# Top-k attention and a squared-ReLU feed-forward on one core: weights in fewer, earlier loads, two early steps changed over sooner, and another order of the tail

## The chip, the core and the metric

The kernel runs on one core of one Trainium2 chip. The metric is the device time of one execution in microseconds (us). The core has five instruction streams that run beside each other and meet at semaphores: PE (TensorE, matrix products, with weight loads shown as PEld), DVE (VectorE), ACT (ScalarE), POOL (GpSimd) and SP (SyncE, which here only issues transfers). Transfers run on 16 DMA engines, which all issuing queues share.

## The reference, cut to what matters

```
scores = q @ k^T / 8                        # 8 batches x 8 heads, 576 rows, 64 wide, float32
kth    = the 32nd largest score of each row
attn   = softmax(scores where scores >= kth)
x      = (attn @ v), heads side by side     # 4608 tokens x 512
h      = relu(x @ w_in)                     # 512 x 2048
out    = (h * h) @ w_out                    # 2048 x 512, float32 out
```

## The kernel before

**Steps.** The 64 heads are taken as 32 pairs (`pairs`). A pair has four 128-row pieces for each head and a rest of 64 rows, and a step works on two such 128-row tiles at once. There are U = 144 steps, numbered u from 0. The loop over u is written out by hand as a pipeline, and every instruction is pinned to program order on its engine (`pin`), so that the order in the code is the order of each queue. A transfer queue is also in order: a transfer that waits holds back the ones behind it.

**One step.** `scores(u+1)` multiplies on PE into two PSUM tiles (`sc_a`, `sc_b`), and ACT copies them to `s` (L294). DVE does the search for the 32nd largest: `pairs_of` (L314, L315, and L317 in early steps) and `quads_of` (L323, L324) sort the 576 scores of a row into maxima and minima of pairs and quads in `cat`; `topk` then runs four rounds of "eight largest" (L374), with the found values replaced after the first three (L378). POOL computes the minima of the pairs from sums (`both` L338, `lesser` L347). `drop(u-1)` on POOL marks the scores below the limit in `gone` (L409) and adds that mark onto `s`, either by a POOL instruction (L411) or by a transfer that accumulates (L413). `exps(u-2)` on ACT (L417) makes the weights `w_two` from `s`, and `turn(u-2)` on SP (L426) transposes them by DMA into `wT`. `products(u-4)` on PE (L461) multiplies with the values, `invert` (L475, DVE) and `place` (L494, ACT) divide by the row sums and write the tokens `x_tok`.

**The constant EARLY (L350).** It is 11. For steps u < EARLY, DVE computes half of the pair minima itself (L317), POOL works on one half only, and ACT doesn't copy the far maxima (`copy_far`, L330). For u < EARLY - 2 the mark of `drop` is added by POOL (L411); from then on by the accumulating transfer (L413).

**Inputs.** `load_pair(i)` lists ten transfers for the q, k and v rows of pair i; `fetch(n)` issues the next n of them on SP. In a step, `fetch(4)` stands behind `turn(u-2)`. `prepare(u)` transposes q and k of the next pair when its due step (`due(i)`) has come: 5, 8, 11 for the pairs 1, 2, 3, each begun four steps ahead. The raw buffers are double.

**Weights.** `w_loads` holds eight loads of 64 partitions for `w_in` and four of 128 partitions for `w_out` (L744). `load_weights` issues them on POOL's queue, converting to bf16: two before `scores(0)`, one behind `lesser(0)`, and one at the end of each of the steps 0 to 8.

**Feed-forward.** When all heads of a 128-token tile are in, PE transposes it (L532), and `block` cuts its work in pieces: four `up` pieces (16 products each, L583, 512 columns of PSUM), each followed by `relu` (ACT, L590) and `square` (ACT L598, or DVE or POOL L596), and 16 products with `w_out` (L649), copied (L657) and stored. Pieces are spread over the steps by `dense`.

**The tail.** The last step's part of the loop (u = U - 2) and all that follows are ordered by hand. Four `up` pieces of the last tile but one (`one`, `two`, `three`, `four`) are left over; its 16 products with `w_out` are issued in parts by `one.bits(n)` (L631). The first two pieces share one PSUM tile of two banks (`two_banks`, named `sc_a`). The last steps' weights are masked on DVE (`mask`, L421), transposed on PE (`turn_by_tensor`, L443) and copied out of PSUM by `turned` (L448 on ACT, L450 on DVE). `tests` are small POOL instructions on `flags` (L384 to L386), which DVE reduces to `worst` (L936). Then the last tile is transposed (L532, copy L536), its four `up` pieces follow with parts of `one.bits` between them, and `halves` multiplies it with `w_out` in two halves (L615), copies them (L621, L623) and stores them (L625).

Of the kernel before, what the change touches and what calls it, by code (L numbers as in the profile page):

```python
# [13 lines left out]
f32 = mybir.dt.float32  # L14
# [9 lines left out]
def kernel(  # L24
# [9 lines left out]
    nc = tc.nc  # L34
# [10 lines left out]
    def pin(ins):  # L45
        tc.keep_in_program_order(ins)
        return ins
# [10 lines left out]
    ps_sc = while_scores.enter_context(tc.tile_pool(name="ps_sc", bufs=1, space=PSUM))  # L58
# [7 lines left out]
    w_in = const.tile([128, KH, d_ff], bf16, name="w_in")  # L66
# [61 lines left out]
    def fetch(n):  # L128
        while n and fetches:
            fetches.pop(0)[1]()  # L130
            n -= 1
# [130 lines left out]
    U = len(steps)  # L262
    first = {}
# [42 lines left out]
    def pairs_of(u):  # L306
# [43 lines left out]
    EARLY = 11  # L350
    held_m = {}
    tests = []

# [43 lines left out]
    def early_exps(u, x):  # L397
        d = st[u]
        if "e" not in d:
            d["e"], d["neg_e"] = {}, negate(u, 1)  # L400
        e = d["e"][x] = scp.tile([128, S], bf16, name="e", bufs=3)
        pin(nc.scalar.activation(e[:, :], d["s"][:, x, :], AF.Exp, bias=d["neg_e"][:, x, 0:1]))
# [12 lines left out]
    def exps(u, x):  # L415
        d = st[u]
        pin(nc.scalar.activation(w_two[u % 3][:, x, 0:S], d["s"][:, x, :], AF.Exp, bias=d["neg"][:, x, 0:1]))  # L417
# [62 lines left out]

    full = []

    def place(u, by_vec=False):
        for x, (i, c, a) in enumerate(steps[u]):
            b, pr = pairs[i]
            o, r = sums(u)[:, x, :], st[u]["r"]
            if c < 4:
                if (b, c) not in x_tok:
                    x_tok[b, c] = ffp.tile([128, 512], bf16, name="x_tok", bufs=8)
                h = 4 * (pr // 2) + 2 * a + pr % 2  # L490
                if by_vec:
# [12 lines left out]


    moves, ups, downs = [], [], []
    soon_moves = []
    late, tail = [], []
# [53 lines left out]
    homes = []  # L562
# [154 lines left out]
    def dense(u, x, later=False):  # L717
        if x == 0:
            ups_now[0] = 0
            while behind:  # L720
                behind.pop(0)()
            while fresh:
                fresh.pop(0)()
        if u in PLAN:
            for kind in PLAN[u][x]:
                take(kind, kind == "d")
            return
        for n in range(2 if u >= U - 20 and x == 0 else 1):
            if not piece(later, most_ups(u)) and n == 0 and shut[0] != u:
                idle_piece()  # L730


    w_loads = []
    for kh in range(KH):
        for e in range(2):
            rows = moe_w_in.rearrange("(t e a d) n -> t a e d n", t=2, e=2, a=2)[kh // 2, kh % 2, e]
            w_loads.append((w_in[64 * e:64 * e + 64, kh, :], rows))
    for g in range(4):
        rows = moe_w_out.rearrange("(f p) n -> p f n", p=128)[:, 4 * g:4 * g + 4, :]
        w_loads.append((w_out[:, 4 * g:4 * g + 4, :], rows))  # L740

    def load_weights(n):
        for to, rows in w_loads[:n]:
            pin(nc.gpsimd.dma_start(out=to, in_=rows))  # L744
        del w_loads[:n]
# [9 lines left out]
    def due(i):  # L755
        if i >= NP - 8:
            return 101 + 4 * (i - (NP - 8))
        return first[4 * (i // 4) + 3] - 1 - 4 * (3 - i % 4) if i >= 4 else 3 * i + 2

    def prepare(u):  # L760
        nonlocal coming
# [14 lines left out]
    load_weights(2)  # L776
    scores(0)
    both(0)
    copy_far(0)
# [8 lines left out]
    def ok(w):  # L788
        return 0 <= w < U
# [6 lines left out]
    def products(w):  # L796
        if ok(w):
            for x in range(2):
                weigh(w, x)
# [6 lines left out]
    for u in range(U):  # L806
        at_step[0] = u
        for x in range(2):
            if ok(u - 1) and not by_vector(u - 1, x):
                drop(u - 1, x)  # L810
        quads_of(u)
        topk(u, (0,))
        if u == U - 1:
            break
        if ok(u + 1):
            for i, c, a in steps[u + 1]:
                while coming <= i or (coming == i + 1 and soon):
# [12 lines left out]
        turn_x(u)  # L830
        moves.extend(soon_moves)
        soon_moves.clear()
        if ok(u - 2):
            exps(u - 2, 0)
            exps(u - 2, 1)
            turn(u - 2)
        fetch(4 if u < 12 else 3)
        topk(u, (1, 2))
        if u == U - 2:
            while behind:  # L840
                behind.pop(0)()
            take("d")
            products(u - 3)
            take("d")
        if ok(u + 1):
            pairs_of(u + 1)
            if u == U - 2:
                invert(u - 3)
            copy_far(u + 1)
            lesser(u + 1)  # L850
            if tests:
                pin(tests.pop(0)())
        if u == U - 2:
            place(u - 3)
            turn_x(u)
            take("d", True)
            early_exps(u, 1)
            moves.pop(0)()()
        topk(u, (3,))
        if casts_next:  # L860
            prepare(u)
        while after_far:
            after_far.pop(0)()
        after_far.extend(next_far)
        next_far.clear()
        if u < U - 2:
            dense(u, 0)
        st[u]["neg"] = negate(u, 2)
        if u < U - 2:
            dense(u, 1)  # L870
        load_weights(1)
# [3 lines left out]
    two_banks = ps_sc.tile([128, 2, 512], f32, name="sc_a")  # L875
    homes.extend(two_banks[:, z, :] for z in range(2))
    one, two = ups.pop(0)(), ups.pop(0)()
    behind.pop(0)()
    one.relu()
    three = ups.pop(0)()  # L880
    products(U - 4)
    four = ups.pop(0)()
    for x in range(2):
        exps(U - 3, x)
    turn(U - 3)
    exps(U - 2, 0)
    one.square(nc.gpsimd)
    two.relu()
    two.square(nc.gpsimd)
    early_exps(U - 1, 0)  # L890
    early_exps(U - 1, 1)
    topk(U - 1, (1, 2, 3))
    one.bits(4)
    three.relu()
    three.square(nc.gpsimd)
    while tests:
        pin(tests.pop(0)())
    mask(U - 2, 1)
    mask(U - 1, 0)
    mask(U - 1, 1)  # L900
# [7 lines left out]
    turned(U - 1, 0, False)  # L908
    products(U - 3)
    turn_by_tensor(U - 1, 1)  # L910
    turned(U - 1, 1, True)
    products(U - 2)
    invert(U - 4)
    invert(U - 3)
    invert(U - 2)
    place(U - 2, True)
    products(U - 1)
    invert(U - 1)
    place(U - 4)
    place(U - 3)  # L920
    place(U - 1, True)
    one.bits(2)
    by_hand.clear()
    late.append(True)
    turn_x(U)
    by_hand.append(True)
    move = moves.pop(0)()
    four.relu()
    late.clear()
    four.square()  # L930
    late.append(True)
    one.bits(2)
    move()
    tail.append(0)
# [4 lines left out]
    fifth.square()  # L939
    sixth = ups.pop(0)()  # L940
    sixth()
    one.bits(4)
    ups.pop(0)()()
    one.bits(4)
    ups.pop(0)()()
# [137 lines left out]
```

## Time and profile before

| | us |
|---|---|
| time, median of 3 runs | 905.44 (904.69 to 906.34) |
| the profiled execution's own time | 910.4 |
| its span, first to last instruction | 908.3 |
| busy: DVE | 878.8 (97%) |
| busy: POOL | 780.7 (86%) |
| busy: ACT | 761.2 (84%) |
| busy: PE | 683.6 (75%) |

The profile is of one execution. The views used are: the page's engine shares, the chain of work that ended last (followed back from the last instruction), the timelines of the engines (start, length, what, and in brackets the idle time before an instruction with what ended it), the windows (busy time of each engine in a stretch, the granted TensorE clock as a share of full speed, the share of the DMA engines, and GB/s), and the list of transfers with the median time from issue to landing. A DMA share over 1 means that packets of several queues stood open on the same engines. The profiled execution is 4.96 us above the median of the timed runs.

### The profile page before, as it was taken

Reading aid. Unit: us, or ns where it says so; the run is one execution under the profiler, and the core shown is the slowest. Engines: PE = TensorE matmul, PEld = TensorE weight load, DVE = VectorE, ACT = ScalarE, POOL = GpSimd, SP = SyncE. Lnnn points to the kernel's source line nnn. Section 1 sums busy time; section 2 is a strip of 40 time slices with the busy share of each in tenths; the row PEclk is TensorE's granted clock in tenths of the full one; section 3 lists DMA queues with packets and bytes.
Section 4 is the critical chain, followed back from the end, with each engine's and each line's share of the span. In section 5 each row is a group of like instructions: output and inputs, shape, how many; then the busy total and the mean of one; then the engine's idle time right before and its main releaser. Section 6 shows DMA issues by size and latency. Waiting matters only on the chain.

```text
span 908.3 us, 20985 instructions
## 1 busy us (share of the span) xinstructions
PE 683.6 (75%) x6264; PEld 426.1 (47%) x6264; DVE 878.8 (97%) x3629; ACT 761.2 (84%) x1755; POOL 780.7 (86%) x821
## 2 busy tenths in 40 slices
PE   6675867777777768777777677787777768887886
PEld 3332445444444445454454444554544444554554
DVE  6998999999999999999999999999999999999994
ACT  3564799889988898888998899888998888997894
POOL 7997889988898888888889888888898898899881
PEclk9999899999999998999998999989999899999998
DMA  7699898889988999899999988989799999787771
GB/s 146 105 165 147 189 187 196 191 193 209 196 189 172 193 206 195 186 184 200 198 190 196 197 195 195 193 194 202 183 202 199 198 205 211 151 169 164 166 162 40
DMA packets 290776, 164.78 MB, mean 181 GB/s; under 512 B 258144, under 2 KB 268640, under 8 KB 290656
## 3 DMA queue, kind: packets, MB, share of 16 engines
q1 hardware_dynamic: 267408, 80.29, 46.2%
q0 software_dynamic: 21904, 82.65, 40.7%
q8 instruction: 52, 0.85, 0.4%
q14 instruction: 68, 0.56, 0.2%
q10 hardware_dynamic: 1344, 0.43, 0.2%
HBM read 37.75 MB, written 9.44 MB: 52 GB/s over the span
## 4 chain that ended last, share of the span: by engine, by line
DVE 62%; issue 12%; ACT 7%; PE 4%; POOL 3%; DMA 2%; POOLq 0%; ACTq 0%
DVE m L374 25%; DVE cat L378 17%; DVE sc_b L314 6%; DVE most L315 4%; DVE cat L323 4%; DVE cat L324 4%; ACT s L294 1%; PE sc_b L285 1%; POOL cat L347 1%; DVE rsum L475 1%; ACT rl L590 1%; ACT x_tok L494 1%; DMA s<-gone_a 1%; ACT w_two_a L417 1%; PE gen L583 1%
## 5 line engine op out<-in xcount | busy, mean ns | idle before, releaser
L374 DVE MAX8 m<-cat 128x8 f32<-128x104 f32 (+3 forms) x1152 | 436.7, 419 | 0.0
L378 DVE MATCH_REPLACE8 cat<-m,cat 128x104 f32<-128x104 f32 (+2 forms) x864 | 261.5, 308 | 0.0
L338 POOL TENSOR_TENSOR cat<-s 128x576 int32<-128x576 int32 (+1 forms) x144 | 238.6, 1657 | 2.8 <-ACT s L294 2.8
L347 POOL TENSOR_TENSOR cat<-cat,most 128x576 int32<-128x576 int32 (+1 forms) x144 | 196.0, 1361 | 31.8 <-ACT most L330 10.7
L285 PE MATMUL sc_b<-qkT 64*128 64x288 f32 x512 | 109.9, 505 | 88.2 <-DVE cat L324 84.1
L285 PE MATMUL sc_a<-qkT 64*128 64x288 f32 x512 | 98.2, 457 | 89.4 <-DVE most L315 35.2
L583 PEld LDWEIGHTS <-w_in 128*128 128x128 bf16 x2304 | 144.8, 101 | 41.7 <-issue 19.0
L649 PE MATMUL dn_ps<-w_out,h 128*128 128x512 bf16 x544 | 155.9, 417 | 1.8 <-ACT wide L657 1.8
L583 PE MATMUL gen<-xT,w_in 128*128 128x128 bf16 x1984 | 135.6, 224 | 3.3 <-ACT xT L538 1.8
L409 POOL TENSOR_SCALAR gone_a<-s,neg 128x576 uint8<-128x576 f32 x143 | 107.1, 749 | 15.5 <-ACT neg L394 4.1
L409 POOL TENSOR_SCALAR gone_b<-s,neg 128x576 uint8<-128x576 f32 x142 | 106.3, 749 | 12.2 <-ACT neg L394 0.3
L294 ACT ACTIVATE s<-sc_b 128x576 f32<-128x576 f32 x144 | 93.4, 648 | 27.8 <-PE sc_b L285 24.0
L285 PEld LDWEIGHTS sc_a<-qkT 64*128 64x128 f32 x512 | 41.6, 188 | 116.8 <-issue 35.4
L294 ACT ACTIVATE s<-sc_a 128x576 f32<-128x576 f32 x144 | 91.3, 634 | 3.2 <-DVE cat L317 1.7
L285 PEld LDWEIGHTS sc_b<-qkT 64*128 64x128 f32 x512 | 45.0, 203 | 103.7 <-PE av_ps L461 62.5
L394 ACT ACTIVATE neg<-m 128x4 f32<-128x4 f32 (+1 forms) x145 | 29.9, 206 | 72.0 <-DVE m L374 70.6
L598 ACT ACTIVATE h<-rl 128x512 bf16<-128x512 f32 x137 | 86.3, 630 | 4.3
L590 ACT ACTIVATE rl<-gen 128x512 f32<-128x512 f32 x140 | 81.9, 585 | 1.8 <-PE gen L583 1.7
L461 PEld LDWEIGHTS <-wT 128*128 128x128 bf16 (+1 forms) x1600 | 55.3, 101 | 57.9 <-issue 45.8
L649 PEld LDWEIGHTS <-h 128*128 128x128 bf16 x544 | 52.5, 106 | 63.5 <-issue 29.9
L413 POOL DMA_DIRECT2D s<-gone_b x67 | 59.3, 885 | 22.0 <-DVE m L374 9.9
L413 POOL DMA_DIRECT2D s<-gone_a x66 | 58.3, 884 | 20.4 <-DVE m L374 10.8
(177 smaller groups left out, 1261.0 us busy)
## 6 DMA issues: line engine op xcount, KB each, us to landing
s<-gone_b POOLq DMA_DIRECT2D x67, 576.0 KB, 4.5
s<-gone_a POOLq DMA_DIRECT2D x66, 576.0 KB, 4.6
v_raw<-in_v_dram SPq DMA_DIRECT2D x64, 128.0 KB, 3.1
k_raw<-in_k_dram SPq DMA_DIRECT2D x63, 128.0 KB, 3.3
q_raw<-in_q_dram SPq DMA_DIRECT2D x63, 128.0 KB, 3.0
out_dram<-wide SPq DMA_DIRECT2D x31, 256.0 KB, 3.0
v_raw<-in_v_dram SPq DMA_DIRECT2D x64, 32.0 KB, 3.0
w_in<-in_moe_w_in_dram POOLq DMA_DIRECT2D x8, 256.0 KB, 4.5
```

Of the source, the lines that this page charges most:

```text
L285: pin(nc.tensor.matmul(out=ps[j][:, x, 0:HALF], lhsT=lhsT, rhs=rhs, start=True, stop=True))
L294: pin(nc.scalar.activation(s[:, :, j * HALF:(j + 1) * HALF], ps[j][:, :, 0:HALF], AF.Copy))
L338: pin(tt(less, s[:, :, 0:wide].bitcast(i32), s[:, :, HALF:HALF + wide].bitcast(i32), op=ALU.add))
L347: pin(tt(less, less, d["most"][:, 0:n_h, :, :].bitcast(i32).rearrange("p h x n -> p x h n"), op=ALU.subtract))
L374: pin(nc.vector.max(out=m[r][:, x, :], in_=part(r, x)))
L378: pin(nc.vector.match_replace(out=part(r, x), in_to_replace=m[r][:, x, :], in_values=part(r, x), imm_value=NEG))
L409: pin(nc.gpsimd.tensor_scalar(byte[:, x, :, 1], s[:, x, :], scalar1=d["neg"][:, x, 1:2], scalar2=-HUGE, op0=ALU.add, op1=ALU.mult))
L413: pin(nc.gpsimd.dma_start(out=s[:, :, :].rearrange("p x n -> p (x n)"), in_=byte[:, :, :, :].rearrange("p x n two -> p (x n two)").bitcast ...
L583: pin(nc.tensor.matmul(out=hp[:, n * n_rows:(n + 1) * n_rows], lhsT=w_in[:, kh, (f0 + n) * 128:(f0 + n + 1) * 128], rhs=xt(kh), start=(kh ...
L590: pin(nc.scalar.activation(kept["rl"][:, :], hp, AF.Relu))
L598: pin(nc.scalar.activation(h2, flat, AF.Square))
L649: pin(nc.tensor.matmul(out=op[:, :], lhsT=held["h2"][:, f, c * 128:(c + 1) * 128], rhs=w_out[:, f, :], start=(f == 0), stop=(f == NF - 1)))
```

## The change

It has four parts.

- **Loads.** `w_in` comes in four loads of 128 partitions and not eight of 64. One load is issued before `scores(0)`, one behind `lesser(0)` and one at the end of the steps 0 to 5, so all eight are out by step 5. In the steps 0 to 5 `fetch(4)` stands ahead of `exps(u-2)` and `turn(u-2)`. The due steps of the pairs 1, 2, 3 are 5, 7, 9.
- **EARLY is 9.** The steps 9 and 10 no longer have L317 on DVE; the marks of the steps 7 and 8 are added by transfer.
- **The first pieces of the tail.** `one` and `two` go to two PSUM tiles (`sc_a`, `sc_b`). `early_exps` of step U - 2 stands behind the last round of `topk`; `exps(U-2, 0)` behind `two.square`; `one.bits(8)` takes the place of `one.bits(4)`.
- **The last steps.** `three.relu`, `three.square` and the `tests` stand behind the products of the last steps, and `four.relu` and `four.square` (on POOL) behind `place`. The second half of the last step's weights is copied by DVE, not ACT; of the last step's two results one is placed by DVE and the other by ACT. `one.bits(4)` between the last tile's second and third `up` piece is gone.

```
--- before.py
+++ after.py
@@ -347,7 +347,7 @@
         pin(tt(less, less, d["most"][:, 0:n_h, :, :].bitcast(i32).rearrange("p h x n -> p x h n"), op=ALU.subtract))
 
     GROUP = 18
-    EARLY = 11
+    EARLY = 9
     held_m = {}
     tests = []
 
@@ -480,7 +480,7 @@
 
     full = []
 
-    def place(u, by_vec=False):
+    def place(u, by_vec=(False, False)):
         for x, (i, c, a) in enumerate(steps[u]):
             b, pr = pairs[i]
             o, r = sums(u)[:, x, :], st[u]["r"]
@@ -488,7 +488,7 @@
                 if (b, c) not in x_tok:
                     x_tok[b, c] = ffp.tile([128, 512], bf16, name="x_tok", bufs=8)
                 h = 4 * (pr // 2) + 2 * a + pr % 2
-                if by_vec:
+                if by_vec[x]:
                     pin(nc.vector.tensor_scalar(x_tok[b, c][:, h * 64:(h + 1) * 64], o[:, 0:64], scalar1=r[:, x, :], scalar2=None, op0=ALU.mult))
                 else:
                     pin(nc.scalar.activation(x_tok[b, c][:, h * 64:(h + 1) * 64], o[:, 0:64], AF.Copy, scale=r[:, x, :]))
@@ -732,9 +732,8 @@
 
     w_loads = []
     for kh in range(KH):
-        for e in range(2):
-            rows = moe_w_in.rearrange("(t e a d) n -> t a e d n", t=2, e=2, a=2)[kh // 2, kh % 2, e]
-            w_loads.append((w_in[64 * e:64 * e + 64, kh, :], rows))
+        rows = moe_w_in.rearrange("(t e a d) n -> t a e d n", t=2, e=2, a=2)[kh // 2, kh % 2]
+        w_loads.append((w_in[:, kh, :], rows))
     for g in range(4):
         rows = moe_w_out.rearrange("(f p) n -> p f n", p=128)[:, 4 * g:4 * g + 4, :]
         w_loads.append((w_out[:, 4 * g:4 * g + 4, :], rows))
@@ -755,7 +754,7 @@
     def due(i):
         if i >= NP - 8:
             return 101 + 4 * (i - (NP - 8))
-        return first[4 * (i // 4) + 3] - 1 - 4 * (3 - i % 4) if i >= 4 else 3 * i + 2
+        return first[4 * (i // 4) + 3] - 1 - 4 * (3 - i % 4) if i >= 4 else 2 * i + 3
 
     def prepare(u):
         nonlocal coming
@@ -773,7 +772,7 @@
     ones = const.tile([128, 1], f32, name="ones")
     pin(nc.gpsimd.memset(ones[:, :], 1.0))
     worst = const.tile([128, 1], f32, name="worst")
-    load_weights(2)
+    load_weights(1)
     scores(0)
     both(0)
     copy_far(0)
@@ -830,11 +829,14 @@
         turn_x(u)
         moves.extend(soon_moves)
         soon_moves.clear()
+        if u < 6:
+            fetch(4)
         if ok(u - 2):
             exps(u - 2, 0)
             exps(u - 2, 1)
             turn(u - 2)
-        fetch(4 if u < 12 else 3)
+        if u >= 6:
+            fetch(4 if u < 12 else 3)
         topk(u, (1, 2))
         if u == U - 2:
             while behind:
@@ -854,7 +856,6 @@
             place(u - 3)
             turn_x(u)
             take("d", True)
-            early_exps(u, 1)
             moves.pop(0)()()
         topk(u, (3,))
         if casts_next:
@@ -868,33 +869,29 @@
         st[u]["neg"] = negate(u, 2)
         if u < U - 2:
             dense(u, 1)
+        else:
+            early_exps(u, 1)
         load_weights(1)
 
     assert len(ups) == 4 and not downs and len(behind) == 1 and not fresh and not moves and not soon_moves
     by_hand.append(True)
-    two_banks = ps_sc.tile([128, 2, 512], f32, name="sc_a")
-    homes.extend(two_banks[:, z, :] for z in range(2))
-    one, two = ups.pop(0)(), ups.pop(0)()
+    homes.extend(ps_sc.tile([128, 2, 512], f32, name=name)[:, 0, :] for name in ("sc_a", "sc_b"))
+    one, two, three = (ups.pop(0)() for _ in range(3))
     behind.pop(0)()
     one.relu()
-    three = ups.pop(0)()
     products(U - 4)
     four = ups.pop(0)()
     for x in range(2):
         exps(U - 3, x)
     turn(U - 3)
-    exps(U - 2, 0)
     one.square(nc.gpsimd)
     two.relu()
     two.square(nc.gpsimd)
+    exps(U - 2, 0)
     early_exps(U - 1, 0)
     early_exps(U - 1, 1)
     topk(U - 1, (1, 2, 3))
-    one.bits(4)
-    three.relu()
-    three.square(nc.gpsimd)
-    while tests:
-        pin(tests.pop(0)())
+    one.bits(8)
     mask(U - 2, 1)
     mask(U - 1, 0)
     mask(U - 1, 1)
@@ -908,27 +905,29 @@
     turned(U - 1, 0, False)
     products(U - 3)
     turn_by_tensor(U - 1, 1)
-    turned(U - 1, 1, True)
+    turned(U - 1, 1, False)
     products(U - 2)
+    products(U - 1)
+    three.relu()
     invert(U - 4)
     invert(U - 3)
-    invert(U - 2)
-    place(U - 2, True)
-    products(U - 1)
-    invert(U - 1)
     place(U - 4)
     place(U - 3)
-    place(U - 1, True)
-    one.bits(2)
+    three.square(nc.gpsimd)
+    while tests:
+        pin(tests.pop(0)())
+    invert(U - 2)
+    place(U - 2, (True, True))
+    invert(U - 1)
+    place(U - 1, (True, False))
+    four.relu()
+    four.square(nc.gpsimd)
     by_hand.clear()
     late.append(True)
     turn_x(U)
     by_hand.append(True)
+    one.bits(2)
     move = moves.pop(0)()
-    four.relu()
-    late.clear()
-    four.square()
-    late.append(True)
     one.bits(2)
     move()
     tail.append(0)
@@ -939,7 +938,6 @@
     fifth.square()
     sixth = ups.pop(0)()
     sixth()
-    one.bits(4)
     ups.pop(0)()()
     one.bits(4)
     ups.pop(0)()()
```

More of the change, by code (lines that the diff above doesn't have):

```diff
@@ L349 @@
     GROUP = 18
-    EARLY = 11
+    EARLY = 9
     held_m = {}
@@ L481, with place @@
     full = []
-    def place(u, by_vec=False):
+    def place(u, by_vec=(False, False)):
         for x, (i, c, a) in enumerate(steps[u]):
@@ L734 @@
     for kh in range(KH):
-        for e in range(2):
-            rows = moe_w_in.rearrange("(t e a d) n -> t a e d n", t=2, e=2, a=2)[kh // 2, kh % 2, e]
-            w_loads.append((w_in[64 * e:64 * e + 64, kh, :], rows))
+        rows = moe_w_in.rearrange("(t e a d) n -> t a e d n", t=2, e=2, a=2)[kh // 2, kh % 2]
+        w_loads.append((w_in[:, kh, :], rows))
     for g in range(4):
@@ L757, in due @@
             return 101 + 4 * (i - (NP - 8))
-        return first[4 * (i // 4) + 3] - 1 - 4 * (3 - i % 4) if i >= 4 else 3 * i + 2
+        return first[4 * (i // 4) + 3] - 1 - 4 * (3 - i % 4) if i >= 4 else 2 * i + 3
     def prepare(u):
@@ L832 @@
         soon_moves.clear()
+        if u < 6:
+            fetch(4)
         if ok(u - 2):
@@ L836 @@
             turn(u - 2)
-        fetch(4 if u < 12 else 3)
+        if u >= 6:
+            fetch(4 if u < 12 else 3)
         topk(u, (1, 2))
@@ L870 @@
             dense(u, 1)
+        else:
+            early_exps(u, 1)
         load_weights(1)
@@ L874 @@
     by_hand.append(True)
-    two_banks = ps_sc.tile([128, 2, 512], f32, name="sc_a")
-    homes.extend(two_banks[:, z, :] for z in range(2))
-    one, two = ups.pop(0)(), ups.pop(0)()
+    homes.extend(ps_sc.tile([128, 2, 512], f32, name=name)[:, 0, :] for name in ("sc_a", "sc_b"))
+    one, two, three = (ups.pop(0)() for _ in range(3))
     behind.pop(0)()
     one.relu()
-    three = ups.pop(0)()
     products(U - 4)
@@ L892 @@
     topk(U - 1, (1, 2, 3))
[L893 to L897, printed above, removed]
+    one.bits(8)
     mask(U - 2, 1)
@@ L910 @@
     turn_by_tensor(U - 1, 1)
-    turned(U - 1, 1, True)
+    turned(U - 1, 1, False)
     products(U - 2)
+    products(U - 1)
+    three.relu()
     invert(U - 4)
     invert(U - 3)
[L915 to L918, printed above, removed]
     place(U - 4)
     place(U - 3)
-    place(U - 1, True)
-    one.bits(2)
+    three.square(nc.gpsimd)
+    while tests:
+        pin(tests.pop(0)())
+    invert(U - 2)
+    place(U - 2, (True, True))
+    invert(U - 1)
+    place(U - 1, (True, False))
+    four.relu()
+    four.square(nc.gpsimd)
     by_hand.clear()
@@ L926 @@
     by_hand.append(True)
+    one.bits(2)
     move = moves.pop(0)()
[L928 to L931, printed above, removed]
     one.bits(2)
@@ L941 @@
     sixth()
-    one.bits(4)
     ups.pop(0)()()
```

7 lines of the change are left out of this document (3 added, 4 removed).

## The prediction

> **What bounds the kernel now.** I read the page first: engine shares and the chain that ended last.
>
> ```profile
> span 908.3 us, 20985 instructions
> PE 683.6 (75%) x6264; PEld 426.1 (47%) x6264; DVE 878.8 (97%) x3629; ACT 761.2 (84%) x1755; POOL 780.7 (86%) x821
> DVE 62%; issue 12%; ACT 7%; PE 4%; POOL 3%; DMA 2%; POOLq 0%; ACTq 0%
> ```
>
> DVE is busy 97% of the span, so in the steps only DVE time counts; what other engines save is worth something only where DVE waits. The span leaves 908.3 - 878.8 = 29.5 us without DVE. The DVE timeline shows where: the start, the tail, and one hole.
>
> ```profile
> 65.46 0.45 DVE L314 TENSOR_TENSOR sc_b<-sc_a,s 128x288 f32<-128x288 f32 x1
> 71.82 0.45 DVE L314 TENSOR_TENSOR sc_b<-sc_a,s 128x288 f32<-128x288 f32 x1
> 78.19 0.45 DVE L314 TENSOR_TENSOR sc_b<-sc_a,s 128x288 f32<-128x288 f32 x1
> 84.18 0.45 DVE L314 TENSOR_TENSOR sc_b<-sc_a,s 128x288 f32<-128x288 f32 x1
> 91.87 0.46 DVE L323 TENSOR_TENSOR cat<-sc_b,most 128x288 f32<-128x288 f32 x1 [5.55 <-ACT most L330]
> ```
>
> The starts of L314 give the period of a step: 71.82 to 78.19 is 6.37 us with L317, 78.19 to 84.18 is 5.99 us without. Then DVE stands 5.55 us. The ACT and POOL timelines tell why:
>
> ```profile
> 90.10 1.44 ACT L417 ACTIVATE w_two_a<-s,neg 128x576 bf16<-128x576 f32 x2 [6.52 <-DMA s<-gone_b]
> 69.91 0.79 POOL L744 DMA_DIRECT2D w_out<-in_moe_w_out_dram  x1
> 78.71 0.95 POOL L413 DMA_DIRECT2D s<-gone_b  x1 [0.31 <-DVE sc_b L314]
> ```
>
> ACT was free at 90.10 - 6.52 = 83.58 and waited for the first accumulating transfer, issued at 78.71. DVE's L323 needs ACT's L330, which queues behind that wait. The lists of transfers, first of the window 76 to 92 us, then of the page, show how late it was; the windows show why.
>
> ```profile
> s<-gone_b POOLq DMA_DIRECT2D x1, 576.0 KB, 11.4
> s<-gone_b POOLq DMA_DIRECT2D x67, 576.0 KB, 4.5
> 20.00:30.00 10.00, 6.49 (x30) 2.79 (x27) 10.00 (x37) 4.97 (x15) 9.41 (x11) 1.00 0.24 36
> 70.00:80.00 10.00, 7.22 (x49) 3.26 (x48) 10.00 (x39) 6.58 (x16) 9.09 (x11) 1.00 1.17 176
> 80.00:90.00 10.00, 4.37 (x28) 2.12 (x24) 6.32 (x26) 2.41 (x8) 6.36 (x6) 0.87 1.25 99
> ```
>
> The last two figures are DMA share and GB/s. The engines idle from 20 to 30 us (0.24) and are overfull from 70 to 90 (1.17, 1.25), with the accumulation landing after 11.4 us, not 4.5.
>
> **The loads.** SP's timeline shows the idle stretch:
>
> ```profile
> 14.05 0.60 SPq L110 DMA_DIRECT2D k_raw<-in_k_dram  x1
> 28.36 1.41 SPq L426 DMA_TRANSPOSE wT<-w_two_a  x1
> ```
>
> From 14.65 to 28.36 SP stands before the first `turn`, with the next `fetch(4)` queued behind. The change lets those loads pass. On POOL the last weight load leaves at the end of step 5, not 8. Its place on POOL's queue can be read off:
>
> ```profile
> 49.59 0.82 POOL L744 DMA_DIRECT2D w_out<-in_moe_w_out_dram  x1
> 12.98 0.53 POOL L744 DMA_DIRECT2D w_in<-in_moe_w_in_dram  x1
> 8.52 1.30 POOL L744 DMA_DIRECT2D w_in<-in_moe_w_in_dram  x2
> ```
>
> The same slot of step 5 starts at 49.59 now, so the last weights leave about 20 us earlier. The first accumulation comes two steps earlier, at 78.71 - 2 x 6.37 = 66.0. The gap between them grows from 78.71 - 69.91 = 8.8 us to about 16. The two pair loads of 4 and 5 also no longer run into each other there: pair 3 begins two steps sooner, so pair 4 is fetched in steps 5 to 7. I take it that the hole goes: -5.5 us in the profiled execution; bounds 0 (it stays) and -5.55.
>
> POOL issues fewer weight instructions, but those of 128 partitions are not in the trace: between 0.53 (one half) and 1.30 (two halves) each; I take 0.8, as `w_out` has with its 128 partitions. Either way POOL holds no one up before step 7, and DVE has no idle time in 20 to 80 us by the windows: cost 0. What is late next, if the loads come too densely, is a transposed `wT` (rival C).
>
> **EARLY 11 to 9.** Two times L317 leaves DVE: 2 x (6.37 - 5.99) = -0.76 us, nothing hides it. In return POOL works on both halves in those steps, ACT does one more copy, and the marks of steps 7 and 8 go by transfer. By form:
>
> ```profile
> 68.30 0.80 POOL L338 TENSOR_TENSOR cat<-s 128x288 int32<-128x288 int32 x1
> 79.37 1.75 POOL L338 TENSOR_TENSOR cat<-s 128x576 int32<-128x576 int32 x1
> 71.61 1.28 POOL L411 TENSOR_TENSOR s<-s,gone_a 128x576 f32<-128x576 f32 x1
> 80.35 0.21 ACT L394 ACTIVATE neg<-m 128x4 f32<-128x4 f32 x1 [1.06 <-DVE m L374]
> ```
>
> POOL pays 0.95 more for L338 (and some 0.6 for L347) and saves two L411 of 1.28 against one L413 of 0.95: about even. ACT has 1.06 us idle in such a step for a copy of 288 columns (512 take 0.49, L538 below). Cost 0; if that cover were gone, up to 0.49 us in each of two steps.
>
> **The tail.** Its critical line is not DVE alone. ACT's, DVE's and POOL's timelines, then the chain:
>
> ```profile
> 883.43 0.60 ACT L590 ACTIVATE rl<-sc_a 128x512 f32<-128x512 f32 x1 [1.45 <-PE sc_a L583]
> 887.44 1.54 DVE L421 SCALAR_TENSOR_TENSOR w_two_c<-s,m,e 128x576 bf16<-128x576 f32 x2 [0.74 <-ACT e L402]
> 888.63 1.25 POOL L596 TENSOR_TENSOR h<-rl 128x512 bf16<-128x512 f32 x1 [1.01 <-ACT rl L590]
> 889.85 0.84 POOL L384 TENSOR_TENSOR flags<-m 128x36 f32<-128x36 f32 x3
> 880.13 0.78 ACT e L402
> 880.91 0.49 ACT xT L538
> 881.45 1.96 PE sc_a L583 x32
> 891.54 0.85 PE dn_ps L631 x2
> 893.50 1.05 PE end L583 x16
> 894.55 0.89 PE gen L583 x16
> 895.45 0.86 PE dn_ps L631 x4
> 899.08 3.61 PE end L615 x32
> ```
>
> *First pieces.* ACT waits 1.45 us because `one.relu` must see both pieces that share a tile: 32 products, 1.96 us. With a tile of its own it needs 16, 0.98 us. L538 also moves ahead of a 0.78 us exponential. So the relu can start about 1.1 us sooner (0.98, and a little of the second, since ACT still has that exponential and a copy ahead of it). The exponentials behind it move with it; DVE's 0.74 us wait before its two last masks closes, and then DVE is late next, since its masks run back to back. Gain at the masks' end: 0.74 to 0.8 us.
>
> *From the masks to the last tile.* Here ACT has one copy less (L448 goes to DVE, L450), and two pairs of relu and square stand later. But the POOL squares and the `tests` now come late too: `worst` on DVE waits for the tests, and the last tile's squares queue behind it. POOL needs 1.25 for `three.square` and about 1.4 for the five tests (0.84 for the first three); with the exponentials 1.1 sooner it starts near 889.0 and is done near 891.7, against 892.3 or later for `worst`: cover of some 0.6 us, and if it is gone, the same amount on the squares. I carry 0.75 of the gain, 0.5 to 1.1, to the start of L583 at 893.50.
>
> *One part less.* The four L631 products (0.86) between the second and third piece go into `one.bits(8)`, at about 885 to 887 us, where PE has gaps. After 893.50 PE runs without a gap up to the end, so the full 0.86 is won, if relu and square of the third piece keep ahead of L615, which comes 0.86 + 0.89 behind that piece. Then -0.75 - 0.86 = -1.6 us, bounds +0.3 and -2.2.
>
> The clock bears on this. Windows again, the granted clock third from the end:
>
> ```profile
> 887.00:889.00 2.00, 0.85 (x13) 0.54 (x11) 1.56 (x3) 2.00 (x4) 0.99 (x2) 1.00 0.89 109
> 891.00:893.00 2.00, 1.97 (x14) 1.02 (x14) 1.12 (x5) 1.91 (x6) 0.25 (x1) 0.53 0.00 0
> 893.00:895.00 2.00, 1.94 (x29) 1.60 (x28) 1.84 (x3) 0.35 (x1) 0.00 (x0) 1.00 0.00 0
> ```
>
> After a stretch with PE busy 0.85 of 2 us the clock is 0.53 at 891 to 893 and full again at 893. I take the same slow stretch before the last tile, now as then. The Trainium skill, "TensorE: Matmul & The Clock Gate", "What's actually happening", says that half clock ends only after about 3.4 us of sustained work in a window that runs freely. By that rule the slow stretch need not move forward with the work, and the last tile's first piece could begin inside it; rival D prices it from the rows.
>
> **The sum.** Against the profiled execution's 910.4: -5.5 - 0.76 - 1.6 = 902.5. The median of the timed runs is 905.44, 4.96 below. A hole of 5.55 us that depends on how the transfers fall would account for nearly all of this difference, so I take the timed runs to hold only 5.5 - 5.0 = 0.5 us of it: 905.44 - 0.5 - 0.76 - 1.6 = 902.6. Forecast 902.6, its own range 901.4 to 903.8.
>
> **The rivals.**
>
> *B. The hole is in the timed runs too.* The 4.96 us would then be a cost of profiling spread elsewhere. For it: the hole follows from a full DMA queue. Against: DVE's steps run back to back in the profile, which leaves little else for 5 us to hide in. Result 905.44 - 5.5 - 0.76 - 1.6 = 897.6. Chance 0.13.
>
> *C. Slower: a transfer comes late in the new order.* Place: the exponentials of step 7 (executed in step 9), the first to need an accumulating transfer. They have 83.58 - 78.71 = 4.9 us in the trace, about 1 us more in the new order as POOL has no weight load (0.82) there; the median landing is 4.5. It decides from about 5.9 us. If the queue is as crowded as at 78.71 (landing 11.4), a hole of up to 5.5 us: 902.6 + 5.5 = 908.1. For it: the accumulation is slow when both queues have work (DMA share 1.25). The Trainium skill, "DMA: Bandwidth & Descriptors", "Queues, rings and completion order", says that each DMA engine takes turns between its queues, packet by packet; so SP's loads lose to POOL's whenever they come together, which the early loads invite. Against: the weights have left 16 us before. Chance 0.14.
>
> *D. The tail gives back its gain.* Half clock reaches the first piece of the last tile: 16 products in 0.89 us at full clock (894.55) become 1.8, and POOL's tests hold `worst` by 0.6. Then the tail gains 1.6 - 0.9 - 0.6 = 0.1: 904.1. For it: the clock row 0.53 ends only at 893. Against: PE has more work ahead of it (`one.bits(8)`). Chance 0.13.
>
> *E. The change does less than it says.* The first hole shrinks but stays at one or two us, or the tail gain is half: 904.5. Chance 0.05.
>
> **How the numbers follow.** Forecast 0.55, B 0.13, C 0.14, D 0.13, E 0.05. A measurement of this kernel tells about 0.2% from no change, 1.8 us: faster is below 903.6, slower above 907.3. The forecast's range lies mostly below 903.6 (0.50 of its 0.55), and so does all of B: faster 0.63. The rest of the forecast (0.05), D, E and a small hole of C (0.04): same 0.27. Slower is the rest of C: 0.10. The range takes in B and leaves out the larger holes of C: 897.3 to 905.8.
>
> **What would show it.** Right: no DVE idle over 1 us between 60 and 100 us; nine L317, not eleven; the first accumulations landing in 4 to 6 us; DMA share above 0.5 in 20 to 30 us; the first relu of the tail without its 1.45 us wait; no wait before the last masks; L583 of the last tile about 9.2 us before the end of L615 now, 8.3 then. Wrong: a wait of ACT for `s<-gone_b` or `gone_a` near 70 us, PE waiting for `wT`, a `worst` that waits for POOL, or a clock below 1.00 while the last tile runs.

## The result and the profile after

The changed kernel is slower: 926.49 us, median of 6 runs (924.19 to 929.02), against 905.29 for the kernel before, run beside it (6 runs, 904.33 to 907.53). The ratio is 1.023, interval 1.0208 to 1.0251: 21.2 us. The forecast was 902.6, range 897.3 to 905.8. The profiled execution of after took 926.36, near its median, so its trace stands for the rest. Of all the runs below one execution is left out of its run's figures as slow: run 8's of 923.22 us.

The page of after, its first lines and the chain by engine (share of the span):

```profile
span 924.3 us, 20902 instructions
PE 680.7 (74%) x6186; PEld 428.1 (46%) x6264; DVE 878.5 (95%) x3627; ACT 760.4 (82%) x1756; POOL 778.0 (84%) x816
DVE 72%; issue 12%; DMA 8%; ACT 4%; PE 3%; SPq 2%; ACTq 0%; DVEq 0%
```

PE, DVE, ACT and POOL work no longer than before: DVE has 878.5 us against 878.8. Only the weight loads that run beside PE (PEld) have 2.0 us more. The span alone grew, by 16.0 us, and the chain now holds 8% of DMA where it held 2%. So time was lost in standing, and DVE's timeline says where:

```profile
60.20 0.17 DVE L475 RECIPROCAL rsum<-av_ps 128x2 f32<-128x2 f32 x1 [22.22 <-PE av_ps L461]
81.33 0.17 DVE L475 RECIPROCAL rsum<-av_ps 128x2 f32<-128x2 f32 x1 [1.95 <-PE av_ps L461]
```

DVE stands for 24.2 us in two holes, and the old hole at L323 is not among them. The account closes: 24.17 - 5.55 = +18.6 of holes, -0.76 for two L317 fewer, -1.7 in the tail, which makes +16.1 against 924.3 - 908.3 = +16.0.

The windows (busy time and count of PE, PEld, DVE, ACT, POOL, then granted clock, DMA share, GB/s) show that nothing was computed for a time:

```profile
20.00:30.00 10.00, 7.93 (x31) 3.28 (x29) 10.00 (x36) 5.08 (x13) 9.31 (x12) 0.83 0.49 92
30.00:40.00 10.00, 2.05 (x9) 1.09 (x8) 7.98 (x34) 2.07 (x5) 7.73 (x9) 0.78 0.91 160
40.00:50.00 10.00, 0.00 (x0) 0.00 (x0) 0.00 (x0) 0.00 (x0) 0.00 (x0) 0.50 1.68 86
50.00:60.00 10.00, 6.37 (x26) 2.93 (x26) 0.00 (x0) 2.67 (x5) 4.03 (x4) 0.67 0.96 77
```

From 40 to 50 us PE with its weight loads, DVE, ACT and POOL have zero instructions. The last figures are the odd ones: the DMA packets take more time (1.68) than in any window shown of before (1.25 at most) while little is moved (86 GB/s). Of the 1.68, SP's queue alone has 114.5% of the 16 engines' time for 0.17 MB and POOL's 53.7% for 0.69 MB, so packets that stand open in one queue are enough for a share over 1. The chain of waits, followed to the end of the hole, and PE's timeline name what was missing:

```profile
12.63 21.85 DMA q_raw<-in_q_dram
34.54 24.85 DMA wT<-w_two_a
```

```profile
34.61 0.63 PE L174 MATMUL gen<-id_f,q_raw 128*128 128x128 f32 x4 [2.44 <-DMA q_raw<-in_q_dram]
50.47 1.12 PE L174 MATMUL gen<-id_f,k_raw 128*128 128x128 f32 x4 [15.23 <-DMA k_raw<-in_k_dram]
59.44 0.73 PE L461 MATMUL av_ps<-vau_a,wT 128*128 128x65 bf16 x10 [3.10 <-DMA wT<-w_two_a]
```

Three transfers of SP come late, one behind the other: inputs of the next pair of heads (`q_raw`, `k_raw`) and the first transposed weights `wT`. SP's timeline (the length is that of the issue) shows that its queue itself stood:

```profile
15.52 10.86 SPq L117 DMA_DIRECT2D q_raw<-in_q_dram  x1
34.54 16.34 SPq L426 DMA_TRANSPOSE wT<-w_two_a  x1
```

The same L426 took 1.41 us to issue before. What stands on the other side is in the list of transfers (count, KB of one, median us from issue to landing), from the page, then of the window 0 to 60 us:

```profile
w_in<-in_moe_w_in_dram POOLq DMA_DIRECT2D x4, 512.0 KB, 24.6
w_out<-in_moe_w_out_dram POOLq DMA_DIRECT2D x2, 512.0 KB, 21.8
wT<-w_two_a SPq DMA_TRANSPOSE x1, 24.9
```

Before, from its page and its window of the same time:

```profile
w_in<-in_moe_w_in_dram POOLq DMA_DIRECT2D x8, 256.0 KB, 4.5
w_out<-in_moe_w_out_dram POOLq DMA_DIRECT2D x4, 512.0 KB, 6.6
wT<-w_two_a SPq DMA_TRANSPOSE x2, 3.3
```

A `w_in` load of 64 partitions landed in 4.5 us; one of 128, twice the bytes, takes 24.6. POOL issued the first and the last of the four at these times:

```profile
8.51 1.04 POOL L743 DMA_DIRECT2D w_in<-in_moe_w_in_dram  x1
23.79 0.83 POOL L743 DMA_DIRECT2D w_in<-in_moe_w_in_dram  x1
```

(the two between, at 13.29 and 16.75, are left out). By the median landing the last is done at 23.79 + 24.6 = 48.4, and PE starts again 2 us behind it, at 50.47. The trace shows one thing more. Software queue (that of POOL's loads) in the window 14 to 16 us, packets, MB, share of 16 engines; after, then before:

```profile
q0 software_dynamic: 795, 0.06, 40.3%
```

```profile
q0 software_dynamic: 23, 0.07, 19.1%
```

About the same bytes, but 795 packets instead of 23. By the packets' sizes in the trace, 15 of the 795 hold 4096 bytes and 780 hold 4; before it was 17 and 6. So the weights themselves travel in packets of 4 KB in both kernels, and the new load adds many of 4 bytes. What these are for, no run shows.

### The profile page after: what moved, and what is told of

Its sections match the earlier page's. It is cut to its first block, busy times and chain, and to the rows that moved or that the text cites. A ratio compares the mean times of both kernels' runs of the same rounds, so it can differ in the third digit from the quotient of the medians.

```text
span 924.3 us, 20902 instructions
## 1 busy us (share of the span) xinstructions
PE 680.7 (74%) x6186; PEld 428.1 (46%) x6264; DVE 878.5 (95%) x3627; ACT 760.4 (82%) x1756; POOL 778.0 (84%) x816
## 4 chain that ended last, share of the span: by engine, by line
DVE 72%; issue 12%; DMA 8%; ACT 4%; PE 3%; SPq 2%; ACTq 0%; DVEq 0%
DVE m L374 30%; DVE cat L378 20%; DVE sc_b L314 6%; DVE most L315 5%; DVE cat L324 5%; DVE cat L323 5%; DMA wT<-w_two_a 4%; DMA q_raw<-in_q_dram 2%; DVE rsum L475 1%; ACT s L294 1%; PE gen L583 1%; ACT rl L590 0%; PE dn_ps L649 0%; SPq L110 0%; DMA k_raw<-in_k_dram 0%
## 5 line engine op out<-in xcount | busy, mean ns | idle before, releaser
L374 DVE MAX8 m<-cat 128x8 f32<-128x104 f32 (+3 forms) x1152 | 436.8, 419 | 0.0
L583 PEld LDWEIGHTS <-w_in 128*128 128x128 bf16 x2304 | 146.4, 101 | 39.4 <-issue 16.6
L649 PE MATMUL dn_ps<-w_out,h 128*128 128x512 bf16 x479 | 141.2, 415 | 8.7 <-issue 4.9
L583 PE MATMUL gen<-xT,w_in 128*128 128x128 bf16 x1984 | 135.5, 224 | 2.3 <-ACT xT L538 1.8
L461 PEld LDWEIGHTS <-wT 128*128 128x128 bf16 (+1 forms) x1600 | 55.3, 101 | 61.1 <-issue 44.6
## 6 DMA issues: line engine op xcount, KB each, us to landing
w_in<-in_moe_w_in_dram POOLq DMA_DIRECT2D x4, 512.0 KB, 24.6
```

The lines of the kernel that those rows point to most:

```text
L374: pin(nc.vector.max(out=m[r][:, x, :], in_=part(r, x)))
L583: pin(nc.tensor.matmul(out=hp[:, n * n_rows:(n + 1) * n_rows], lhsT=w_in[:, kh, (f0 + n) * 128:(f0 + n + 1) * 128], rhs=xt(kh), start=(kh ...
L649: pin(nc.tensor.matmul(out=op[:, :], lhsT=held["h2"][:, f, c * 128:(c + 1) * 128], rhs=w_out[:, f, :], start=(f == 0), stop=(f == NF - 1)))
```

## The experiments

**Theory after the result.** The source of a 128-partition `w_in` load is two runs of 64 rows (`e` and `d` of the rearranged array, once `t` and `a` are fixed). The Trainium skill, "DMA: Bandwidth & Descriptors", "Why a DMA increments its semaphore by 16 and not by 1", says that a DMA is spread over the largest number k of engines, at most 16, that divides the slowest dimension of both its sides. With a source of two runs and 128 partitions k would be 2; with 64 rows and 64 partitions it is 16. The section also names exceptions for some copies from this kind of queue, so whether the rule holds here is for the runs. By it, two engines then carry the load for 24 us, and whatever SP spreads over all of them waits for those two. Rivals: the size of the load; four large loads set too closely; the new order or the tail. The profile's views do not list the DMA engines one by one, so the theory is tested by the shape, and by how much of the 16 engines' time the software queue takes. All ratios below are to the kernel before, run in the same rounds on the same chip.

### 1. The same loads at the same times, each in two halves

```
- w_loads.append((w_in[:, kh, :], rows))
+ w_loads.append([(w_in[64*e:64*e+64, kh, :], rows[e]) for e in range(2)])
```

All else is as in after; a slot now issues both halves back to back.

> The changed kernel, with each w_in load as two loads of 64 partitions, both issued where the one was; all else as changed. Theory (few engines: the 128-partition load, whose source is two runs of 64 rows, is spread over few of the 16 DMA engines): loads land after about 5 us as before, not 24.6, the idle of DVE at 38 to 60 us is gone, and the time is 905.3 - 0.5 - 0.76 - 1.73 = 902.3 us. Rival (crowding: weights and fetches that come earlier fill the queues, whatever their shape): the same bytes at the same places, so 920 us or more. Rival (size: one transfer of 512 KB is too long): about 902 too.

902.94 us, ratio 0.9981 (0.9965 to 0.9997). L475 waits 1.4 us for `av_ps` in the whole execution, 0.8 at the longest, where after has 25.2 and 22.2. The list of its transfers:

```profile
w_in<-in_moe_w_in_dram POOLq DMA_DIRECT2D x8, 256.0 KB, 6.1
```

The same bytes leave in the same slots, and the 22 us are gone. It is neither the schedule of the loads nor the tail.

### 2. Full size, but a source that is one run

```
- rows = moe_w_in.rearrange("(t e a d) n -> t a e d n", t=2, e=2, a=2)[kh // 2, kh % 2]
- w_loads.append((w_in[:, kh, :], rows))
+ w_loads.append((w_in[:, kh, :], moe_w_in[128*kh:128*kh+128, :]))
```

> The changed kernel, with each w_in load of 128 partitions reading 128 rows in one run and not two runs of 64 (so the first product is with other rows than the reference's); size, count and places as changed. Few engines: landing after 5 to 8 us, 902.3 us. Size and crowding: as the changed kernel, about 926 us.

902.21 us, ratio 0.9967 (0.9954 to 0.998). The list:

```profile
w_in<-in_moe_w_in_dram POOLq DMA_DIRECT2D x4, 512.0 KB, 6.9
```

Still 128 partitions and 512 KB, but 6.9 us instead of 24.6. So size and partitions aren't the cause; the split source is. (The first product takes other rows than the reference's; the instructions and the bytes are the same.)

### 3. The large load alone in the kernel before

```
- for e in range(2):
-     rows = ...[kh // 2, kh % 2, e]
-     w_loads.append((w_in[64*e:64*e+64, kh, :], rows))
+ rows = ...[kh // 2, kh % 2]
+ w_loads.append((w_in[:, kh, :], rows))
+ w_loads.append(None)     # the second half's slot stays empty
```

> The kernel before, with only the shape changed: the first of each two w_in slots issues the load of 128 partitions, the second issues nothing; fetch order, EARLY and tail as before. Few engines: the four loads land after 15 us or more and DVE waits, 908 to 925 us. Crowding: the same bytes at about the same time, so 905 us within 1.5. Size: as few engines.

933.03 us, ratio 1.031 (1.0289 to 1.0331): the sign is as expected, and the cost is above the expected range. Its DVE timeline and its list of transfers (the last row of the window 0 to 60 us):

```profile
52.68 0.17 DVE L475 RECIPROCAL rsum<-av_ps 128x2 f32<-128x2 f32 x1 [15.00 <-PE av_ps L461]
72.57 0.17 DVE L475 RECIPROCAL rsum<-av_ps 128x2 f32<-128x2 f32 x1 [13.44 <-PE av_ps L461]
```

```profile
w_in<-in_moe_w_in_dram POOLq DMA_DIRECT2D x4, 512.0 KB, 25.8
wT<-w_two_b SPq DMA_TRANSPOSE x1, 25.0
```

The shape of the load brings the whole loss by itself. It is larger here: the last of the four loads leaves at 36.30 us, not at 23.79, and there are two long holes, one behind the other, where in after the four loads overlap ahead of one.

### 4. Halves by columns: half the bytes, the same two runs

```
+ w_loads.append([(w_in[:, kh, 1024*z:1024*z+1024], rows[:, :, 1024*z:1024*z+1024]) for z in range(2)])
```

> The changed kernel, with each w_in load as two loads of 128 partitions by 1024 columns, both issued where the one was, so each as large as a load of the kernel before but with the two runs of the changed one. Few engines: both halves share the same few engines, the second lands after about 24 us, and the time is 920 to 932 us. Size: landing after 5 to 7 us and 902 to 904.

914.51 us, ratio 1.0081 (1.0053 to 1.0109). Its list and its DVE timeline:

```profile
w_in<-in_moe_w_in_dram POOLq DMA_DIRECT2D x8, 256.0 KB, 16.7
```

```profile
45.99 0.17 DVE L475 RECIPROCAL rsum<-av_ps 128x2 f32<-128x2 f32 x1 [7.97 <-PE av_ps L461]
```

256 KB in 16.7 us, where 256 KB by rows take 6.1: size as the cause falls once more. But my own 920 to 932 fell too. I had taken both halves to share the same engines and to last as long together as one load. They landed sooner, which fits halves on different engines; the Trainium skill says, in the same section, that this kind of queue moves on from one load to the next around the engines. The trace of after agrees. From 28 to 30 us, with its four loads of two runs in flight, the software queue has about half of the 16 engines' time, 8.2 engines' worth or two to a load:

```profile
q0 software_dynamic: 50, 0.20, 51.3%
```

That this is why the column halves landed sooner is not tested by itself.

### 5. and 6. The number of runs as a dose

Four loads of 128 partitions whose source has 2, 4, 8 and 16 runs, put into the kernel before at the ends of steps 0, 2, 4 and 6; then in reverse order. The rows of `w_in` are other ones.

```
+ g = (2, 4, 8, 16)[kh]          # second run: (16, 8, 4, 2)
+ rows = moe_w_in.rearrange("(g h d) n -> h g d n", g=g, h=4)[h]
```

> The kernel before with four w_in loads of 128 partitions, one at the end of each of the steps 0, 2, 4, 6, whose source is 2, 4, 8 and 16 runs of rows (so the first product is with other rows than the reference's), and w_out in the steps 8 to 11. Few engines, as many as divide the number of runs: with 24.6 us for 2 runs and 6.9 for one run of 128 rows (16 engines) as the ends of a + b/k, a = 4.4 and b = 40, so landing after about 24, 14, 9 and 7 us. Rival (two runs far apart in memory are slow by themselves, as are more of them): 24 us or more for all four. Rival (only the crowd of the first 30 us makes it slow): falling with the step, but not in this ratio.

One profile, 932.51 us: 23.3, 22.8, 10.8 and 5.5 us in order of issue. The second is off: it was issued at 29.88 us, while the first, issued at 16.55, was not done until 39.9. From 30 to 39 us the software queue has 12.4% of the 16 engines' time, two engines' worth, so the second hardly moved beside the first, unlike the loads in after. The fourth load of run 3, issued with the third in flight, waited in the same way and took 33.9 us. Why these two waited stays open. A dose behind a larger dose can't be read, so I turned the order round.

> As the kernel with 2, 4, 8 and 16 runs, in the reverse order: 16, 8, 4, 2 at the end of the steps 0, 2, 4, 6 (rows in another order than the reference's). There 23.3, 22.8, 10.8 and 5.5 us were measured, and the second was issued while the first still had 10 us to go. Few engines: the number follows the runs and not the step, and no load stands behind an unfinished one: about 7, 9, 13 and 23 us. Rival (the crowd that eases with time): the first is again the slowest.

One profile, 943.03 us. Its lists of the windows 16 to 18, 29 to 31, 40 to 47 and 60 to 75 us:

```profile
w_in<-in_moe_w_in_dram POOLq DMA_DIRECT2D x1, 512.0 KB, 5.5
w_in<-in_moe_w_in_dram POOLq DMA_DIRECT2D x1, 512.0 KB, 9.7
w_in<-in_moe_w_in_dram POOLq DMA_DIRECT2D x1, 512.0 KB, 13.2
w_in<-in_moe_w_in_dram POOLq DMA_DIRECT2D x1, 512.0 KB, 25.2
```

16, 8, 4 and 2 runs of the same 512 KB: the landing follows about 2.8 + 44/k us (5.6, 8.3, 13.8 and 24.8 by that fit of mine). A number of engines equal to the number of runs would do this, and the share of the software queue says the same. These are its rows for four windows inside the four landings: 19 to 21, 33 to 38, 45 to 55 and 66 to 74 us.

```profile
q0 software_dynamic: 93, 0.38, 96.0%
q0 software_dynamic: 111, 0.45, 46.5%
q0 software_dynamic: 118, 0.48, 24.4%
q0 software_dynamic: 48, 0.20, 12.1%
```

Of 16 engines these are 15.4, 7.4, 3.9 and 1.9, for 16, 8, 4 and 2 runs: a load of two runs keeps two engines' worth of time busy and no more. The holes follow the dose too, in DVE's timeline, behind the loads of 8, 4 and 2 runs (issued at 29.91, 42.59 and 61.79):

```profile
45.39 0.17 DVE L475 RECIPROCAL rsum<-av_ps 128x2 f32<-128x2 f32 x1 [1.22 <-PE av_ps L461]
57.67 0.17 DVE L475 RECIPROCAL rsum<-av_ps 128x2 f32<-128x2 f32 x1 [5.82 <-PE av_ps L461]
91.12 0.17 DVE L475 RECIPROCAL rsum<-av_ps 128x2 f32<-128x2 f32 x1 [14.27 <-PE av_ps L461]
```

### 7. to 11. The other parts, one by one

*7. Only the earlier loads and fetches, 64 partitions each* (two halves a slot, as in run 1; EARLY 11; tail of before):

```
- return ... if i >= 4 else 3 * i + 2
+ return ... if i >= 4 else 2 * i + 3
+ if u < 6:
+     fetch(4)      # now ahead of the turns
```

> Only the order of the loads is changed (weights and fetches earlier, due steps 5, 7, 9), w_in in loads of 64 partitions, two a slot; EARLY 11 and the tail as before. If earlier loads are worth something by themselves, it is the hole of the first accumulations: the profiled execution of the kernel before had 5.5 us of it, that of the tail alone 0.3. So 904.7 - 0.5 = 904.2 if the timed runs hold little of it; 902 or less if the timed runs hold more; 906 or more if the crowd of the first 60 us costs DVE time.

904.54 us (903.22 to 906.13), ratio 0.9967 (0.9938 to 0.9996). In the rounds that this run shares with runs 4 and 8, and in no others, the kernel before fell in two clusters: 17 of 29 executions took 902.6 to 906.4 us, 12 took 908.8 to 914.5. None of the 12 of this kernel is in the upper one. That fits a hole like the one of 5.55 us that comes and goes in before, and that the earlier loads remove; those executions were not profiled, so it is argued, not shown. The ratios of runs 4 and 8 are to this scattered kernel before as well.

*8. Only EARLY* (`EARLY = 9` in the kernel before):

> The kernel before with EARLY 9 and nothing else changed. By the count of L317 two instructions leave DVE, 0.76 us: 904.7 - 0.8 = 903.9 us if the earlier accumulating transfers find room behind the last weight loads. Rival (the two steps of lead were needed because the last weight load leaves at 69.9 us and the first accumulation would now meet it): a hole of 2 to 6 us, 906 to 910.

908.72 us (11 executions, 906.41 to 916.08), ratio 1.0038 (1.0003 to 1.0072): not better, rather worse. The waits of the window 60 to 110 us (total, times, longest):

```profile
DVE cat L323 <- ACT most L330: 3.2, 2, 1.8
ACT w_two_b L417 <- DMA s<-gone_b: 2.5, 1, 2.5
```

With the old loads the first accumulation now comes two steps sooner and still late, so the two L317 less bring nothing here.

*9. Only the tail*:

```
+ early_exps(u, 1)     # behind the first pieces, no more ahead of the last step's weights
- two_banks = ps_sc.tile([128, 2, 512], f32, name="sc_a")
+ homes.extend(ps_sc.tile([128, 2, 512], f32, name=name)[:, 0, :] for name in ("sc_a", "sc_b"))
+ one, two, three = (ups.pop(0)() for _ in range(3))
```

> The kernel before with only the changed tail (the first pieces in two PSUM tiles and the order of the last steps); loads and EARLY as before. From the two traces the stretch from the last topk's end to the last copy shrinks from 18.16 to 16.43 us: 905.3 - 1.7 = 903.6 us. Rival (the tail's gain in the changed kernel came from DMA engines left idle by the shifted loads): 905.3.

904.04 us, ratio 0.9995 (0.9984 to 1.0007): inconclusive, the interval goes from -1.4 to +0.6 us. Its trace, which has the loads of before, has no wait of L323 over 0.30 us: the hole of 5.55 us is not in every execution with these loads.

*10. Loads and tail, EARLY 11* (run 1 with `EARLY = 11`):

> The changed kernel with w_in in loads of 64 partitions, two a slot, and EARLY back at 11. Against the same with EARLY 9 (run beside it) two L317 more on DVE: 0.76 us slower if the earlier accumulations cost nothing; as fast or faster if they bring back part of the hole (the profile of the first such run had 1.6 us of it).

902.57 us, ratio 0.9975 (0.9963 to 0.9986).

*11. Loads and EARLY, the tail of before* (run 1 with the old tail):

> The changed kernel with w_in in loads of 64 partitions, two a slot, and the tail of the kernel before. Against the same with the changed tail (run beside it) 1.7 us slower by the two traces; 0.7 by the times of the run with the tail alone.

903.73 us, ratio 0.9992 (0.9979 to 1.0005).

### 12. The kernel of run 1 once more, beside runs 10 and 11

> The changed kernel with w_in in loads of 64 partitions, two a slot, again and in more rounds, beside the two that lack one part each: 902 to 903 us, 2 to 3 us under the kernel before where that has no hole in its executions, more where it has.

901.00 us (899.41 to 905.61), ratio 0.9969 (0.9953 to 0.9985). Beside it, taking the tail back costs 2.7 us (903.73) and taking EARLY back 1.6 us (902.57), but the executions overlap (899.41 to 905.61 here, 902.45 to 908.26 and 900.52 to 904.26 there). This version, everything of the change but the large `w_in` loads, was below the kernel before in both of its measurements, by 1.7 and 2.8 us by the ratios, and its medians are 23.6 and 25.5 us below that of after, which was measured in other rounds.

## Why the prediction was wrong

**The step that failed: the price of the large loads.** The prediction costed "those of 128 partitions" by their issue on POOL alone, "between 0.53 (one half) and 1.30 (two halves) each", and closed with "cost 0". The issue was right (0.83). The landing was left out, 24.6 us instead of 4.5, and that accounts for the error in the time: runs 1 and 2 give the same schedule without it at 902.94 and 902.21, where 902.6 had been forecast. The trace of before had `w_out` with 128 partitions at 6.6 us, and I took it as the like of the new load when I priced the issue. It is alike in partitions and bytes, not in the source: the diff drops the index `e`, and two runs of 64 rows remain. A transfer that the trace doesn't show has two unknowns, issue and landing; I bounded one. The bound on the other would have had to come from the shape of both sides.

**"What is late next ... is a transposed wT (rival C)."** It was `wT` that came late, but not there. Rival C put it at step 7, for a crowded queue, at up to 5.5 us. It came at the first turn, from a few engines held by a long load, at 22.2. The list of signs had it, without a price: PE waiting for `wT` stands among the signs of being wrong, and PE's L461 shows it. The chance of 0.10 for slower was worked out from that one place.

**The rule of the Trainium skill that I weighed.** Rival C drew on turns between queues, packet by packet ("DMA: Bandwidth & Descriptors", "Queues, rings and completion order"), and feared them where many loads come together. The trace of run 3 agrees with turns, but no crowd is needed. From 40 to 44 us a load of two runs holds two engines' worth of time, and while SP's `wT` waits, one packet of SP's queue goes for each of POOL's:

```profile
q0 software_dynamic: 24, 0.10, 12.1%
q1 hardware_dynamic: 24, 0.01, 1.1%
```

A packet of POOL's is 4 KB and lasts 0.32 us in the trace, one of SP's 256 bytes and 0.03 us. So what of `wT` is left for these two engines goes at the pace of the weights: in run 3 it took 25.0 us although the large loads lie further apart there. The prediction had the turns and lacked the number of engines that a load gets.

**The hole goes: right.** In after the first accumulating transfers landed in 4.7 and 4.9 us by its list of the window 55 to 110 us:

```profile
s<-gone_b POOLq DMA_DIRECT2D x2, 576.0 KB, 4.7
s<-gone_a POOLq DMA_DIRECT2D x2, 576.0 KB, 4.9
```

No wait of L323 is left in its DVE timeline there. The long stall ahead of it gives the queue time to empty, so run 12, which has no stall, is the fairer witness: it has no such wait in its first 110 us either. But an accumulating transfer can be late elsewhere: in run 12 ACT waits 3.53 us for `s<-gone_a` up to 380.82, far behind the last weight load, and L323 then 2.60. That timed runs hold little of the hole of before fits most rounds; in those of run 7, 12 of 29 executions may hold it.

**EARLY: right in the count, not shown in the time.** Nine L317 instead of eleven, by the groups of after:

```profile
L317 DVE TENSOR_TENSOR cat<-sc_a,s 128x288 f32<-128x288 f32 x9 | 4.0, 447 | 0.0
```

Forecast -0.76; the medians of runs 10 and 12 differ by 1.6, but their executions overlap, so no run here shows the size. Alone it gains nothing (run 8): the step leans on the earlier loads, which the prediction did not say.

**The tail: right in the traces.** From the last MAX8 to the last copy before: 884.56 (L374) to 902.72 (L621), 18.16 us. After, from DVE's, PE's and ACT's timelines:

```profile
902.19 1.41 DVE L374 MAX8 m<-cat 128x8 f32<-128x576 f32 x2
904.67 1.53 DVE L421 SCALAR_TENSOR_TENSOR w_two_c<-s,m,e 128x576 bf16<-128x576 f32 x2
910.11 1.34 DVE L935 TENSOR_REDUCE worst<-flags 128x1 f32<-128x1152 f32 x1
```

```profile
910.25 1.05 PE L583 MATMUL end<-xT,w_in 128*128 128x128 bf16 x16
```

```profile
900.61 0.59 ACT L590 ACTIVATE rl<-sc_a 128x512 f32<-128x512 f32 x1
918.62 0.38 ACT L621 ACTIVATE wide<-end 128x256 f32<-128x256 f32 x1 [2.61 <-PE end L615]
```

902.19 to 918.62 is 16.43: -1.73 against -1.6. By its two parts, up to L583 it was 893.50 - 884.56 = 8.94 and is 8.06 (-0.88 against -0.75), from there to L621 9.22 and now 8.37 (-0.85 against -0.86). The first relu has lost its 1.45 us wait, the last masks their 0.74, and `worst` waits for no one. The granted clock is 1.00 in every window from 905 to 918 us, so rival D did not come. The other traces agree: 16.27 us in run 9 and 15.80 in run 12 with the new tail, 18.02 in run 11 with the old. The times leave the size open, from run 9's interval (-1.4 to +0.6) to the 2.7 between runs 11 and 12.

## What to carry to other kernels

When two loads are merged into one, look at the shape of what is left on both sides, not at partitions and bytes: a slowest dimension of 2 made a load of 512 KB last 24.6 us where one of 128 rows took 6.9. Price a transfer by issue and landing, and ask what else needs the DMA engines that it holds. In a profile, a queue that stays near 12% of the 16 engines' time while a load of 512 KB is in flight points to such a load, even where the chain names another queue's transfer.

## What the runs showed of the hardware

A load from POOL's queue with a source of 16, 8, 4 and 2 runs landed in 5.5, 9.7, 13.2 and 25.2 us at equal bytes, and the queue had 96.0, 46.5, 24.4 and 12.1% of the 16 engines' time meanwhile. One such load of two runs holds up another queue: SP's `wT` took 24.9 us instead of 3.3, and its issue 16.34 instead of 1.41, and packets of the two queues left one for one (24 and 24 in 4 us of run 3). A gain can also need its neighbour: EARLY 9 without the earlier loads was slower by 0.3 to 6.5 us, by the interval of its ratio; with them no loss is seen. What the 4-byte packets of the split loads are, why one load waited for the other in runs 3 and 5, and what makes the kernel before fall in two clusters in some rounds and in one in the others stay open.
